# A sketched linear attention feeding a channel mix: k rows turned at unit stride, v in four loads, held loads, whole stationaries, and a new issue order

## The chip, the core and the metric

The kernel runs on one core of a Trainium2 chip. A core has five engines with a queue each, which run in their own order and meet only at semaphores: PE (matrix products, with a separate row for loading the stationary operand, PEld), DVE (vector), ACT (scalar functions), POOL (GpSimd) and SP (which here only starts transfers). A queue's instructions run in the order in which the program lists them. The metric is the time of one execution on the device in microseconds (us).

## What is computed

Four batches of four heads, 1088 positions, head width 32, sketch size 8. An attention with a product feature map, and a channel mix over its output:

```python
def phi(x):                       # (.., 32) -> (.., 64)
    a = np.einsum('rd,bhsd->bhsr', S1, x)
    b = np.einsum('rd,bhsd->bhsr', S2, x)
    return np.einsum('bhsi,bhsj->bhsij', a, b).reshape(*x.shape[:-1], r * r)
q_p, k_p = phi(q), phi(k)
kv, z = np.einsum('bhsf,bhsd->bhfd', k_p, v), np.sum(k_p, axis=2)
num = np.einsum('bhsf,bhfd->bhsd', q_p, kv)
den = np.einsum('bhsf,bhf->bhs', q_p, z)[..., None] + 1e-06
x = (num / den)                   # heads side by side: (4, 1088, 128)

x_prev = shift of x by one position, zero in front
xk, xr = mu_k * x + (1 - mu_k) * x_prev, mu_r * x + (1 - mu_r) * x_prev
k = np.maximum(xk @ w_k, 0.0)     # 128 -> 1024
out = 1 / (1 + np.exp(-(xr @ w_r))) * ((k * k) @ w_v)
```

## The kernel before

The program is a list of small tasks. Each is a Python function, and the string `ORDER` names them in the order in which they are issued; an engine runs its share of that list in list order. An entry such as `abev.0.1.A` is task, batch, part and engine (A for ACT, V for DVE, G for POOL, P for DVE reading straight from PSUM), and the digits behind `@` are the PSUM banks it writes. All eight banks are one tile; the framework inserts the semaphore waits for everything that shares a tile's region, a buffer or a bank.

Per batch, the attention goes through these tasks:

- `kt` (L260): DVE turns the k rows in 32x32 blocks, half a batch at a time, into `kT`; `qt` (L264) does the same for q.
- `kproj` (L269): PE projects the turned k with both sketches. `abev` copies the result to SBUF, `kp` (DVE or POOL) forms the 64 products of a position.
- `zmm`, `zev`, `wmm`, `wsq`: the sum over positions, folded into a third column block of `SQ[b]`, the right-hand side of q's projection, so that the denominator comes out of the same matmuls.
- `abw` (L346): PE projects q with `SQ[b]`: part `q` the two sketches, `w` the denominator's column, `f` all three. `pw` and `den` make the reciprocal of the denominator, `an` scales, `qp` forms the products.
- `kvmm`, `kvev`, `kdmm`, `kdev`: kv from `kp` and v, copied and turned into `kvw`.
- `pt`, `ptev`, `xp`, `xpev` (and `tt`, `ttev`, `xt`, `xtev` for the last two positions of each 34; `tr`, `xn`, `xnev` in the last batch): the q products turned and multiplied with kv, into `X32`, the channel mix's input.

The channel mix works in nine groups, two per batch and one (8) of the remainders of all batches: `xk` and `xr` mix with the position before; `f1` (L505) is the first matmul, in four parts of a pair of banks each, `relu` its activation, `sq` the square, `f2` the second matmul, `rr` and `sig` the gate, `fin` the product, `st` the store. `f1` and `xp` write two banks, which `pair` (L101) addresses as `PS[:, i:j + 1:j - i, :n]`, a strided region from the first bank to the last. In `st` the queues S and A are SP's and ACT's; with `SA` four transfers are shared between the two.

`muset` (L226) prepares the mixing coefficients with six small DVE instructions (L227 to L232). `wkset`, `wvset` and `wrset` cast the weights. `zz` are matmuls on zeros into a bank that is free, for PE's clock.

The loads are all started by SP in the order of the string `LOADS` before anything else on its queue, the small ones by ACT. k and q come as rows of 34 positions, one row per partition, 32 partitions per head; k's first load is in two halves. v comes in two loads per batch, to every second partition (L132 to L136). With k turned into `kT[P, 9, 32, 4]` at a stride of four elements, position 34a + 9c.. sits at column 4a + c, and v lies at the same partitions:

```python
nc.vector.transpose(_ap(kT[b % 2][:, 0, 0], [[1, 2], [128, 9], [4, 32]], 2 * y), ...)   # kt
d = o[32 * i:32 * i + 32, 32 * (m - m0):32 * (m - m0) + 32]                            # kproj, i in 0..3
kT[b % 2][:, m, 8 * i:8 * i + 8]                                                       # its stationary, 32 columns
```

In `kproj` and `abw` each group of 128 positions is projected by four matmuls whose stationaries have 32 columns, one for each strip of 32 output partitions.

Of the kernel before, what the change touches and what calls it, by code (L numbers as in the profile page):

```python
# [39 lines left out]
pt.1.1.1@7 kt.3.1 kproj.3.0@1 fin.0 kproj.3.1@0 abev.3.1.A f1.1.3@26 den.2.0.36 abev.3.0.A xk.0.2.G sq.1.0.V xr.0.1.V  # L40
kvmm.2.0@5 ptev.1.0.0.A relu.1.3.A an.2.0.36.G kp.3.1.G ptev.1.1.1.V zmm.3@7 zev.3.A kvmm.2.1 kvev.2.A xt.1 xp.1.0@04
sq.1.3.A xp.1.1@26 qt.3.1 kp.3.0.P wmm.3 xpev.1.0.A xtev.1.A qt.3.0 wsq.3 f2.1.0@1 sq.1.1.A xs.1.A abw.3.0.f@7
abwev.3.0.f.A xpev.1.1.V xk.1.1.P abw.3.1.f@3 xk.1.0.P rr.1@2 sig.1 f1.3.0@67 qp.2.20.36.G xr.1.0.P f2.1.1 f1.2.3@04
abwev.3.1.f.V f2.1.2 qp.2.0.20.G f1.2.0@23 relu.3.0.A relu.2.3.A f2.1.3 pw.3.0.36.V f1.3.1@67 sq.3.0.V pt.2.0.1@0
sq.2.3.V relu.2.0.A fin.1 xk.1.2.G xr.1.2.V kdmm.2 f1.3.2@23 sq.2.0.V den.3.0.36 relu.3.1.A f1.3.3@14 kdev.2.V
pt.2.0.0@6 ptev.2.0.0.V relu.3.2.A pt.2.1.1@7 f1.2.2@23 pt.2.1.0@5 relu.3.3.A f1.2.1@14 tt.2@6 ptev.2.1.1.V relu.2.2.A
ptev.2.1.0.A ptev.2.0.1.V relu.2.1.A ttev.2.V st.1.S kvmm.3.0@7 sq.3.2.V sq.3.1.A xp.2.0@05 sq.3.3.V xp.2.1@23
xpev.2.1.A xt.2 kvmm.3.1 xpev.2.0.V xtev.2.V sq.2.1.A rr.2@1 sig.2 xr.1.1.G f2.3.0@6 rr.3@4 an.3.0.36.G xs.2.V
qp.3.0.20.G kvev.3.V sig.3 xk.2.1.P f2.3.1 f1.5.0@23 relu.5.0.A xk.2.0.P xr.2.0.P xr.2.1.V f2.3.2 f1.5.2@14 sq.2.2.V
f2.3.3 fin.3 xk.2.2.G qp.3.20.36.G f1.4.0@23 relu.5.2.A f2.2.0@0 tr.3.0 kdmm.3 relu.4.0.A f1.4.3@16 relu.4.3.A f2.2.1  # L50
f1.4.2@23 f2.2.2 kdev.3.V xn.3.0@4567 sq.5.0.V tr.3.1 rr.5@1 f2.2.3 fin.2 relu.4.2.A f1.5.1@23 xnev.3.0.A xs.3.G
xk.3.0.V xn.3.1@4567 sq.5.2.V rr.4@0 sig.5 f2.5.0@1 relu.5.1.A f1.4.1@23 sq.5.1.V sq.4.0.V xnev.3.1.A f1.6.0@45
sq.4.3.V f1.5.3@67 sig.4 relu.4.1.A sq.4.1.V relu.5.3.A f2.5.1 st.3.S f2.4.0@0 relu.6.0.A f1.6.3@23 relu.6.3.A
xk.3.2.V f2.5.2 f1.6.2@67 sq.5.3.V f2.5.3 st.0.S f2.4.1 f1.6.1@45 sq.4.2.V relu.6.2.A xk.3.1.V fin.5 relu.6.1.A
# [555 lines left out]
```

## Time and profile before

| | us |
|---|---|
| runs before, median of 3 | 117.89 (117.11 to 118.21) |
| the profiled execution | 118.51 |
| its span in the profile | 116.7 |
| PE busy | 83.2 |
| DVE busy | 77.2 |
| ACT busy | 63.8 |
| POOL busy | 46.5 |

The span runs from the first recorded instruction to the last. Busy times are unions of instruction durations on one engine. In rows in order of time the columns are the start, the duration, the engine, the line, the operation, output and inputs with their shapes, the number of instructions merged in the row, and in brackets the idle time of that engine just before and what ended it. In rows by line stand the total busy time and the mean duration in ns, then the idle time before. `ACTq` and `SPq` rows are the issuing of transfers on those queues. A line can be that of a helper: L258 is every elementwise product, L251 and L255 the copies on ACT and DVE.

### The profile page before, as it was taken

Reading aid. Unit: us, or ns where it says so; the run is one execution under the profiler, and the core shown is the slowest. Engines: PE = TensorE matmul, PEld = TensorE weight load, DVE = VectorE, ACT = ScalarE, POOL = GpSimd, SP = SyncE. Lnnn points to the kernel's source line nnn. Section 1 sums busy time; section 2 is a strip of 40 time slices with the busy share of each in tenths; the row PEclk is TensorE's granted clock in tenths of the full one; section 3 lists DMA queues with packets and bytes.
Section 4 is the critical chain, followed back from the end, with each engine's and each line's share of the span. In section 5 each row is a group of like instructions: output and inputs, shape, how many; then the busy total and the mean of one; then the engine's idle time right before and its main releaser. Section 6 shows DMA issues by size and latency. Waiting matters only on the chain.

```text
span 116.7 us, 3943 instructions
## 1 busy us (share of the span) xinstructions
PE 83.2 (71%) x1720; PEld 60.9 (52%) x1731; DVE 77.2 (66%) x128; ACT 63.8 (55%) x93; POOL 46.5 (40%) x64
## 2 busy tenths in 40 slices
PE   5898391897199770877678369796298989968640
PEld 2294371776159650846556146466176656637540
DVE  4759987373783513961996459756696499996440
ACT  2212100269445775237857439797356899768450
POOL 6319341058649900150599900825200498000000
PEclk9999859589755999779999999999967999999999
DMA  3899999910000000000000001300015000145404
GB/s 106 268 318 402 389 397 388 370 51 6 0 6 0 0 8 0 0 0 6 3 6 6 0 0 22 68 6 3 6 34 133 19 0 0 27 102 132 102 5 132
DMA packets 9860, 10.27 MB, mean 88 GB/s; under 512 B 882, under 2 KB 7284, under 8 KB 9844
## 3 DMA queue, kind: packets, MB, share of 16 engines
q1 hardware_dynamic: 9232, 9.77, 25.8%
q10 hardware_dynamic: 612, 0.27, 1.0%
q8 instruction: 13, 0.21, 0.7%
q14 instruction: 3, 0.02, 0.1%
HBM read 7.80 MB, written 2.23 MB: 86 GB/s over the span
## 4 chain that ended last, share of the span: by engine, by line
PE 22%; DVE 17%; ACT 11%; SPq 4%; issue 3%; DMA 1%; ACTq 1%; DVEq 0%
ACT k L519 7%; PE ps L540 7%; DVE k L258 5%; PE ps L513 5%; SPq L568 4%; PE ps L431 3%; DVE q L558 3%; DVE xk L483 3%; PE ps L549 2%; DVE X L255 2%; ACT q L555 2%; PE ps L440 1%; DMA out_dram<-q 1%; DVE xr L483 1%; DVE xk L486 1%
## 5 line engine op out<-in xcount | busy, mean ns | idle before, releaser
L519 ACT ACTIVATE k<-ps 128x1024 bf16<-128x1024 f32 (+1 forms) x36 | 33.9, 976 | 18.7 <-PE ps L513 9.3
L540 PE MATMUL ps<-wv,k 128*128 128x128 bf16 x272 | 21.7, 227 | 7.2 <-ACT k L519 5.1
L540 PEld LDWEIGHTS <-k 128*128 128x128 bf16 x272 | 18.4, 102 | 13.9 <-issue 9.4
L513 PE MATMUL ps<-xk,wk 128*128 128x512 bf16 x54 | 18.0, 413 | 6.9 <-ACT k L519 3.2
L258 DVE TENSOR_TENSOR k<-k 128x1024 bf16<-128x1024 bf16 (+1 forms) x26 | 17.3, 701 | 4.0 <-ACT k L519 4.0
L258 POOL TENSOR_TENSOR qp<-an,abw 128x1280 f32<-128x1280 f32 (+3 forms) x9 | 16.6, 1857 | 0.2
L258 POOL TENSOR_TENSOR kp<-ab 128x1024 f32<-128x1024 f32 (+1 forms) x5 | 10.6, 2131 | 7.7 <-ACT ab L251 7.7
L513 PEld LDWEIGHTS <-wk 128*128 128x128 bf16 x72 | 6.4, 103 | 9.1 <-issue 5.2
L258 POOL TENSOR_TENSOR an<-abw,den 128x288 f32<-128x288 f32 (+2 forms) x5 | 3.3, 651 | 19.3 <-DVE den L384 13.0
L558 DVE TENSOR_TENSOR q<-ps,q 128x512 f32<-128x512 f32 (+1 forms) x9 | 5.9, 658 | 7.2 <-PE ps L540 3.6
L276 PE MATMUL ps<-SK,kT 128*32 128x64 f32 x288 | 7.7, 285 | 3.5 <-issue 2.8
L356 PE MATMUL ps<-SQ,qT 128*32 128x96 f32 (+2 forms) x360 | 8.3, 247 | 2.5 <-DVE SQ L314 2.0
L261 DVE STREAM_TRANSPOSE kT<-kv 128x576 f32<-128x576 f32 x8 | 9.4, 1194 | 1.0 <-DMA kv<-in_k_dram 1.0
L528 ACT ACTIVATE k<-k 128x1024 bf16<-128x1024 bf16 (+1 forms) x10 | 9.9, 1014 | 0.1
L276 PEld LDWEIGHTS ps<-SK,kT 128*32 128x32 f32 x288 | 6.8, 154 | 3.9 <-issue 2.9
L356 PEld LDWEIGHTS ps<-SQ,qT 128*32 128x32 f32 x360 | 6.9, 120 | 3.7 <-DVE SQ L314 2.6
L251 ACT COPY ab<-ps 128x320 f32<-128x320 f32 (+1 forms) x8 | 3.1, 400 | 10.2 <-PE ps L276 10.2
L431 PE MATMUL ps<-ident,qp 128*128 128x128 f32 x48 | 8.7, 324 | 0.1
L431 PEld LDWEIGHTS ps<-ident,qp 128*128 128x128 f32 x48 | 7.0, 170 | 1.5 <-issue 0.7
L483 DVE SCALAR_TENSOR_TENSOR xk<-ps,rat,X 128x512 bf16<-128x512 f32 x6 | 4.5, 750 | 4.6 <-ACT k L519 1.7
L258 DVE TENSOR_TENSOR kp<-ps,ab 128x1280 f32<-128x1280 f32 x3 | 4.4, 1476 | 4.6 <-ACT ab L251 4.6
L323 PE MATMUL ps<-kp,kv 128*32 128x64 f32 x288 | 6.8, 245 | 0.0
(95 smaller groups left out, 120.4 us busy)
## 6 DMA issues: line engine op xcount, KB each, us to landing
q<-in_q_dram SPq DMA_DIRECT2D x4, 544.0 KB, 7.7
out_dram<-q SPq DMA_DIRECT2D x28, 64.0 KB, 1.8
kv<-in_k_dram SPq DMA_DIRECT2D x3, 544.0 KB, 6.6
kv<-in_v_dram SPq DMA_DIRECT2D x4, 288.0 KB, 6.8
kv<-in_v_dram SPq DMA_DIRECT2D x4, 256.0 KB, 7.5
kv<-in_k_dram SPq DMA_DIRECT2D x2, 272.0 KB, 2.9
wk_f<-in_moe_w_k_dram SPq DMA_DIRECT2D x1, 512.0 KB, 9.2
wv_f<-in_moe_w_v_dram SPq DMA_DIRECT2D x1, 512.0 KB, 9.4
```

The lines of the kernel that those rows point to most:

```text
L258: (nc.gpsimd if eng == "G" else nc.vector).tensor_mul(o, x, y)
L261: nc.vector.transpose(_ap(kT[b % 2][:, 0, 0], [[1, 2], [128, 9], [4, 32]], 2 * y), kin[b][:, y].rearrange("p (c m d) -> p c m d", c=2, m=9))
L276: nc.tensor.matmul(_ap(d, [[n, 2], [1, 32]]), kT[b % 2][:, m, 8 * i:8 * i + 8].rearrange("p a c -> p (a c)"), SK[:].rearrange("p x h r -> ...
L323: nc.tensor.matmul(o[32 * h:32 * h + 32, :F], vin[b][:, h, m, :], sb["kp", b, j][:, 4 * (m - KG[j][0]) + h].rearrange("p i j -> p (i j)"), ...
L356: nc.tensor.matmul(_ap(o[32 * c:32 * c + 32], [[w * step, H], [1, w]], w * i0), qT[b % 2][:, 4 * t + c, :], SQ[b][:, :, R * x0:R * x1], sk ...
L431: nc.tensor.transpose(o[:, P * h:P * h + P], x.rearrange("p y i j -> p (y i j)"), ident[:])
L483: nc.vector.scalar_tensor_tensor(o.rearrange("p (y n) -> p y n", y=2), ps["xp", b, g], rat[:, i:i + 1], x[:, u:u + n].rearrange("p (y n) - ...
L513: nc.tensor.matmul(h[:, c, :], wk[:, 2 * cp + c].rearrange("p y f -> p (y f)"), x, skip_group_check=True)
L519: nc.scalar.activation(o[:, :, :size(g)], h, RELU)
L528: nc.scalar.activation(o[:, :, :n], k1[:, :, :n], mybir.ActivationFunctionType.Square)
L540: nc.tensor.matmul(o[:, i * P:i * P + P], k2[:, c, i * P:i * P + P], wv[:, 2 * cp + c, :], start=(cp == 0 and c == 0 and i == 0), stop=(cp ...
L558: nc.vector.tensor_mul(osb(g), ps["o", g][:, :size(g)], osb(g))
```

## The change

Four edits in the functions, and a new list of tasks.

`kT` becomes `[P, 9, 4, 32]` and `kt` writes 32 elements at unit stride, so that column 32c + a holds row a of chunk c. v is laid out to match: chunk c goes to partitions 32c to 32c+31 in a load of its own, four per batch in the order 0, 2, 1, 3.

An entry of `LOADS` with a plus sign is no load but a transfer of four bytes out of the named tile into `held`: SP can issue it only when that tile's load has landed, and what stands behind it on SP's queue is issued after it.

`kproj` and `abw` take a letter: T as before, four stationaries of 32 columns; W, one of 128 columns. Two of eight `kproj` and three of ten `abw` have W: `kproj.0.1`, `kproj.1.0`, `abw.0.1.q`, `abw.0.1.w` and `abw.1.1.f`, together 21 groups of positions.

```diff
-LOADS = "k0 q0 v0 k1 q1 w0 v1 w1 w2 k2 q2 v2 k3 q3 v3"
+LOADS = "k0 q0 k1 v0 +k1 q1 w0 +v0 v1 w1 w2 +v1 k2 q2 +q2 v2 k3 +v2 q3 v3"
...
     def load_v(b):
-        s = v[b].rearrange("h (p u) d -> p h u d", u=U // 2)
-        for y in range(2):
-            nc.sync.dma_start(vin[b][y::2, :, :9 - y, :].rearrange("p h m d -> p h (m d)"),
-                              s[:, :, 9 * y:17 if y else 9, :].rearrange("p h m d -> p h (m d)"))
+        s = v[b].rearrange("h (a u) d -> a h u d", u=U)
+        for c in (0, 2, 1, 3):
+            n = 9 - c % 2
+            nc.sync.dma_start(vin[b][32 * c:32 * c + 32, :, :n, :].rearrange("p h m d -> p h (m d)"),
+                              s[:, :, CU[c]:CU[c] + n, :].rearrange("a h m d -> a h (m d)"))
...
+    held = const.tile([1, 32], F32)
+    for i, x in enumerate(LOADS.split()):
+        x, b = x[-2], int(x[-1])
+        if LOADS.split()[i][0] == "+":
+            src = {"k": kin, "q": qin}[x][b][:1, 1, :1] if x in "kq" else vin[b][96:97, 0, 0, :1]
+            nc.sync.dma_start(held[:, i:i + 1], src)
+        elif x == "k":
...
-    kT = [const.tile([P, 9, 32, 4], F32, name=f"kT{i}") for i in range(2)]
+    kT = [const.tile([P, 9, 4, 32], F32, name=f"kT{i}") for i in range(2)]
...
-        nc.vector.transpose(_ap(kT[b % 2][:, 0, 0], [[1, 2], [128, 9], [4, 32]], 2 * y),
+        nc.vector.transpose(_ap(kT[b % 2][:, 0, 2 * y], [[32, 2], [128, 9], [1, 32]]),
...
+        w = 32 if how == "T" else P
         for m in range(m0, m1):
-            for i in range(4):
+            for i in range(0, P, w):
...
+                nc.tensor.matmul(_ap(o[i:i + w, 32 * (m - m0):32 * (m - m0) + 32], [[n, 2], [1, 32]]),
+                                 kT[b % 2][:, m].rearrange("p c a -> p (c a)")[:, i:i + w],
                                  SK[:].rearrange("p x h r -> p x (h r)"), skip_group_check=True,
-                                 tile_position=(0, 32 * i))
+                                 tile_position=(0, i) if w == 32 else None)
```

`abw` is changed in the same way. Of the list, 397 entries long (398 before), these are the parts of which the prediction speaks: the start, the feed-forward of batch 0, and the end.

```diff
-kt.0.0 zz.5@7 smm@0 sset zz.3@1 mumm@0 kt.0.1 zmu@1 kproj.0.0@2 abev.0.0.A kproj.0.1@3 abev.0.1.A sqset zset qt.0.1
-qt.0.0 zz.2@1 zmm.0@3 zev.0.A zz.1@2 wmm.0 abw.0.0.q@2 abwev.0.0.q.A kp.0.0.G muset wsq.0 abw.0.1.w@3 abw.0.0.w@0
-kt.1.1 kp.0.1.G pw.0.0.20.P den.0.0.20 abw.0.1.q@2 kvmm.0.0@1 zz.1@0 kvmm.0.1 kvev.0.A an.0.0.20.G kt.1.0 kproj.1.0@0
-abev.1.0.A qp.0.0.8.V qt.1.0 kproj.1.1@4 abev.1.1.A abwev.0.1.q.V qp.0.8.20.G kdmm.0 kp.1.1.G pt.0.0.0@5 ptev.0.0.0.A
...
-ttev.0.V pw.0.20.36.P den.0.20.36 an.0.20.36.G xp.0.0@46 xpev.0.0.A xt.0 xtev.0.V abw.1.0.f@3 abwev.1.0.f.A
-abw.1.1.f@2 abwev.1.1.f.A xs.0.G xk.0.0.P f1.0.0@05 xr.0.0.P qp.0.20.28.G relu.0.0.A f1.0.2@37 qp.0.28.36.G
...
-relu.0.3.A sq.0.1.A sq.0.3.A abw.2.1.f@2 kp.2.1.G abw.2.0.f@6 wvset.1.V sq.0.2.A kdev.1.A xpev.0.1.V xk.0.1.P
-abwev.2.0.f.V kt.3.0 tt.1@3 f2.0.1 pt.1.0.1@0 abwev.2.1.f.V pw.2.0.36.G ttev.1.V ptev.1.0.1.A xr.0.2.G pt.1.1.0@6
...
-st.6.SA f1.8.1@67 relu.8.1.A sq.8.1.V f1.8.3@15 rr.7@2 sig.7 f2.7.2 f2.8.0@6 sq.8.2.V relu.8.3.A sq.8.3.A f2.7.3 fin.7
-f2.8.1 xr.2.2.G rr.8@2 sig.8 st.7.SA f2.8.2 f2.8.3 fin.8 st.8.S
+zz.6@7 smm@0 kt.0.0 zmu@1 sset sqset kt.0.1 zz.1@2 mumm@0 muset kproj.0.0.T@2 abev.0.0.V qt.0.0 zset qt.0.1
+kproj.0.1.W@3 abev.0.1.A zz.2@0 zmm.0@3 zev.0.A zz.1@2 wmm.0 kp.0.0.G kp.0.1.G abw.0.1.q.W@1 kt.1.0 abw.0.0.q.T@2
+abwev.0.0.q.A wsq.0 abw.0.0.w.T@3 abwev.0.1.q.A kt.1.1 kproj.1.1.T@0 abev.1.1.A abw.0.1.w.W@2 pw.0.0.20.P den.0.0.20
+an.0.0.20.G qp.0.0.8.G kproj.1.0.W@1 abev.1.0.A kp.1.1.P qt.1.1 kvmm.0.0@0 pw.0.20.36.P den.0.20.36 qp.0.8.20.G
...
+wkset.0.A abw.1.1.f.W@1 abwev.1.0.f.A kdev.0.V wkset.1.V wvset.1.V pt.0.0.1@4 abwev.1.1.f.A pw.1.0.36.V ptev.0.0.0.A
+ptev.0.0.1.A den.1.0.36 an.0.20.36.G kt.2.1 qp.0.20.28.G qp.0.28.36.G pt.0.1.0@0 ptev.0.1.0.A pt.0.1.1@1 ptev.0.1.1.A
+wrset.G xt.0 xtev.0.A kt.2.0 xs.0.A xp.0.0@24 xpev.0.0.A kvmm.1.0@5 xp.0.1@01 xpev.0.1.A kvmm.1.1 kproj.2.0.T@3
+abev.2.0.A xk.0.0.P f1.0.1@24 kproj.2.1.T@6 wvset.0.G xk.0.1.P xr.0.1.P abev.2.1.V f1.1.0@37 relu.0.1.A relu.1.0.A
+kvev.1.V qt.2.1 an.1.0.36.G qp.1.0.20.G qp.1.20.36.G f1.1.2@01 relu.1.2.A f1.1.1@24 qt.2.0 kp.2.0.G pt.1.0.1@6
+ptev.1.0.1.V zmm.2@3 zev.2.V sq.1.0.A relu.1.1.A pt.1.0.0@7 sq.0.1.A kdmm.1 kdev.1.A f1.0.0@01 kt.3.0 wmm.2 wsq.2
...
+xr.3.0.G st.5.S sq.8.0.V rr.6@5 sig.6 sig.7 fin.6 st.6.SA f2.7.1 f1.8.3@17 f1.8.2@36 relu.8.2.A f2.7.2 f2.8.0@5
+sq.8.2.V f2.7.3 fin.7 st.7.SA xr.2.2.G relu.8.3.A f2.8.1 rr.8@3 f2.8.2 sq.8.3.A f2.8.3 sig.8 fin.8 st.8.S
```

More of the change, by code (lines that the diff above doesn't have):

```diff
@@ L40 @@
[L40 to L54, printed above, removed]
@@ new lines @@
+pt.1.1.0@6 kt.3.1 abw.2.0.f.T@3 relu.0.0.A ptev.1.0.0.V ptev.1.1.0.V f1.0.2@24 relu.0.2.A abwev.2.0.f.V pt.1.1.1@7
+ptev.1.1.1.V abw.2.1.f.T@5 abwev.2.1.f.V xk.0.2.V f1.0.3@36 relu.0.3.A kproj.3.0.T@0 kp.2.1.G f1.1.3@57 f2.1.0@2
+qt.3.0 pw.2.0.36.G qt.3.1 kproj.3.1.T@4 sq.0.2.V abev.3.0.A rr.1@3 sq.1.2.V relu.1.3.A abev.3.1.A tt.1@6 kvmm.2.0@1
+zmm.3@4 sq.1.1.A ttev.1.A kvmm.2.1 sig.1 kvev.2.A xp.1.0@57 xr.0.0.V zev.3.V xt.1 xtev.1.A den.2.0.36 xpev.1.0.V
+xs.1.A sq.1.3.A wmm.3 f2.1.1 wsq.3 rr.0@6 f2.1.2 sig.0 xk.1.0.P kp.3.1.G abw.3.0.f.T@4 xr.0.2.G sq.0.0.A xr.1.0.P
@@ new lines @@
+ptev.2.1.1.V relu.3.2.A sq.3.0.A kvev.3.V xt.2 xtev.2.V pt.2.1.0@7 ptev.2.1.0.A f2.2.0@4 f1.3.1@26 relu.3.1.A
+qp.3.20.36.G f2.2.1 xpev.2.0.V xs.2.V xp.2.1@57 xk.2.0.P f1.4.1@13 xpev.2.1.A relu.4.1.A kdmm.3 f2.2.2 tr.3.0
+f1.4.0@57 relu.4.0.A kdev.3.V tr.3.1 f2.2.3 fin.2 xn.3.0@0123 xk.2.1.G xnev.3.0.A f1.4.2@57 f2.3.0@6 sq.3.3.V xs.3.G
+rr.3@0 relu.4.2.A sq.3.1.V xn.3.1@1234 sig.3 f1.5.0@57 sq.4.0.V xnev.3.1.A f2.3.1 f1.4.3@12 relu.5.0.A sq.3.2.V
+relu.4.3.A f2.3.2 f1.5.1@57 relu.5.1.A f2.3.3 sq.4.1.V sq.4.2.V f1.5.2@34 f2.4.0@1 xk.3.0.V fin.3 st.3.S f1.5.3@02
@@ L267, with kproj @@
     KG = ((0, 5), (5, 9))
-    def kproj(b, j, banks):
+    def kproj(b, j, how, banks):
         o = ps["ab", b, j] = PS[:, banks[0], :]
@@ L347, with abw @@
     S0 = (0, 20, 36)
-    def abw(b, g, part, banks):
+    def abw(b, g, part, how, banks):
         o = ps["abw", b, g, part] = PS[:, banks[0], :]
```

33 lines of the change are left out of this document (17 added, 16 removed).

## The prediction

> **What bounds the kernel now.** I read the page's sums first, then the busy time by stage, the order of time, and last the rows by line.
>
> ```profile
> span 116.7 us, 3943 instructions
> PE 83.2 (71%) x1720; PEld 60.9 (52%) x1731; DVE 77.2 (66%) x128; ACT 63.8 (55%) x93; POOL 46.5 (40%) x64
> core 0: us, PE busy (x) PEld busy (x) DVE busy (x) ACT busy (x) POOL busy (x), PEclk, DMA share, GB/s
> 3.50:28.60 25.10, 19.24 (x568) 15.02 (x569) 18.22 (x30) 6.84 (x16) 11.04 (x16) 0.86 0.82 294
> 30.00:70.00 40.00, 26.94 (x597) 20.21 (x601) 24.15 (x36) 22.90 (x35) 20.30 (x20) 0.87 0.01 2
> 75.00:110.00 35.00, 28.39 (x492) 20.26 (x496) 26.29 (x42) 25.65 (x34) 10.49 (x11) 0.95 0.18 41
> ```
>
> No engine fills the span. PE is busy 81% of the stage from 75 to 110 us (28.39 of 35), 67% from 30 to 70 (26.94 of 40). So the end is set by waits between engines, and mostly by those of the first 70 us. The order of time shows two of them.
>
> ```profile
> 8.42 4.31 POOL L258 TENSOR_TENSOR kp<-ab 128x1280 f32<-128x1280 f32 x2 [2.68 <-ACT ab L251]
> 8.75 2.10 DVE L228 TENSOR_SCALAR omu<-mu 128x2 f32<-128x2 f32 x1
> 10.88 1.88 DVE L229 TENSOR_SCALAR tmp<-omu 128x2 f32<-128x2 f32 x1
> 12.79 0.16 DVE L230 TENSOR_TENSOR omu<-omu,tmp 128x2 f32<-128x2 f32 x1
> 13.26 0.18 DVE L314 TENSOR_TENSOR SQ<-ps,m 128x32 f32<-128x32 f32 x1
> 16.04 0.46 POOL L258 TENSOR_TENSOR an<-abw,den 128x160 f32<-128x160 f32 x1 [3.31 <-DVE den L384]
> 28.65 0.75 DVE L483 SCALAR_TENSOR_TENSOR xk<-ps,rat,X 128x512 bf16<-128x512 f32 x1 [1.60 <-ACT X L251]
> 29.45 0.38 PE L513 MATMUL ps<-xk,wk 128*128 128x512 bf16 x1 [1.10 <-DVE xk L483]
> ```
>
> The first: two DVE instructions on two elements (muset, L228 and L229) take 2.10 and 1.88 us, where their neighbour L230 takes 0.16. They end at 10.85 and 12.76; POOL's two kp run from 8.42 to 12.73. They stood still while POOL worked, 3.98 - 2x0.16 = 3.7 us, and wsq (L314) with pw, den and POOL's an came behind them. The first feed-forward matmul (f1, L513) starts only at 29.45.
>
> ```profile
> 42.37 2.94 ACT L528 ACTIVATE k<-k 128x1024 bf16<-128x1024 bf16 x3
> 45.21 0.25 ACT L251 COPY kvw<-ps 128x128 f32<-128x128 f32 x1
> 45.50 0.69 DVE L255 COPY X<-ps 128x512 f32<-128x512 f32 x1 [4.18 <-ACT kvw L251]
> 46.23 0.75 DVE L483 SCALAR_TENSOR_TENSOR xk<-ps,rat,X 128x512 bf16<-128x512 f32 x1
> 47.12 0.38 PE L450 MATMUL ps<-ident,qp 64*64 64x64 f32 x4 [3.56 <-DVE xk L483]
> 49.14 0.80 POOL L258 TENSOR_TENSOR pw<-abw 128x288 f32<-128x288 f32 x1 [8.40 <-DVE abw L255]
> ```
>
> The second: three squares hold ACT, kdev.1 waits behind them, and then DVE idles 4.18 us, PE 3.56 and POOL 8.40. xpev.0.1 (DVE, banks 0 and 4) waits for kdev.1 (bank 1), with which it shares no bank, and tt.1 (PE, bank 3) for the reader of 0 and 4. From this I take it that a pair of banks keeps out whatever touches a bank between the two.
>
> **The front.** The new order puts muset ahead of the first kproj, hence ahead of POOL's first kp: the 3.7 us of DVE go, on the path to an. These rows price what else changes there:
>
> ```profile
> L261 DVE STREAM_TRANSPOSE kT<-kv 128x576 f32<-128x576 f32 x8 | 9.4, 1194 | 1.0 <-DMA kv<-in_k_dram 1.0
> L265 DVE STREAM_TRANSPOSE qT<-q 128x544 f32<-128x544 f32 x8 | 5.7, 723 | 0.3 <-DMA q<-in_q_dram 0.3
> L258 DVE TENSOR_TENSOR kp<-ps,ab 128x1280 f32<-128x1280 f32 x3 | 4.4, 1476 | 4.6 <-ACT ab L251 4.6
> L258 DVE TENSOR_TENSOR qp<-an,abw 128x512 f32<-128x512 f32 x1 | 1.8, 1814 | 0.0
> L255 DVE CAST wv<-wv_f 128x512 bf16<-128x512 f32 x1 | 0.4, 417 | 0.0
> L258 DVE TENSOR_TENSOR pw<-abw 128x288 f32<-128x288 f32 x1 | 0.5, 457 | 0.0
> L276 PE MATMUL ps<-SK,kT 128*32 128x64 f32 x288 | 7.7, 285 | 3.5 <-issue 2.8 <-ACT k L519 0.7
> L310 PE MATMUL ps<-zs,ZL 128*128 128x32 f32 x8 | 1.4, 260 | 0.0
> ```
>
> A k turn writes at a stride of four elements and takes 1194 ns for 576; a q turn writes at unit stride and takes 723 for 544. At unit stride the k turn should take 723x576/544 = 765, a saving of 0.43 us. No row shows that block shape, so the saving lies between 0 and 0.43; I take 0.43, as the q turn differs in little else.
> DVE's list up to xk.0.0, L483 at 28.65: it loses muset's 3.7, four dearer turns (1.7) and qp.0.0.8, which goes to POOL (1.8). It gains kp.1.1 from POOL (1476x1024/1280 = 1.2), two turns of batch 2 (1.5), wkset.1 and wvset.1 (0.4 each by the cast), pw.1 (0.46) and den.1 (an estimate of 0.9, two instructions of pw's size or so). That is -7.2 + 4.9 = -2.3. The old front was 25.1 us with DVE busy 18.2, so 6.9 of gaps. With the old gaps xk.0.0 comes 2.3 us earlier. But the old list made DVE wait for POOL and ACT behind the stalled muset, and what it waited for now starts 3.7 us earlier; with gaps of 4 it is 5.2. I take **-4**.
>
> Beside that path: 21 projection units run with one whole stationary instead of four strips. Four strips cost 7.7 us/36 = 0.21 us of PE a unit; the nearest whole fp32 stationary, L310, costs two instructions of 1.4/8 us, 0.35 a unit. That bounds the addition at 21x0.14 = 3 us, and from below at about -1 if fewer instructions help. PE has 5.9 us of gaps in that stage, and most of the units wait for DVE. I take 0; without the gaps it is up to +1 on the path. POOL takes qp.0.0.8 in its gaps (11.04 busy of 25.1). wkset.1 on DVE could stand still behind a POOL instruction as muset did: 0 to 1 us; POOL should be through qp by then.
>
> **The loads.** Five reads of four bytes each hold SP until a load has landed, and queued behind each are the next k, q, v and w loads; v is issued in four pieces.
>
> ```profile
> 9.27 0.56 SPq L130 DMA_DIRECT2D kv<-in_k_dram  x1
> 11.82 3.26 SPq L135 DMA_DIRECT2D kv<-in_v_dram  x2
> L135 SPq DMA_DIRECT2D kv<-in_v_dram x8: 612/615/672, 2.4 to 18.0; - x8
> kv<-in_k_dram SPq DMA_DIRECT2D x3, 544.0 KB, 6.6
> kv<-in_k_dram SPq DMA_DIRECT2D x2, 272.0 KB, 2.9
> 12.00:24.00 12.00, 7.68 (x271) 6.46 (x272) 8.93 (x16) 1.16 (x4) 3.64 (x4) 0.72 1.01 371
> ```
>
> k1 moves ahead of v0, 544 KB at 371 GB/s or 1.5 us earlier. A hold costs nothing if another load is still in flight, at most the 2.9 us from issue to landing on an empty queue. Four pieces at 0.615 take SP 2.5 us for 544 KB that the queue moves in 1.5, so 1 us more for a v. k2, issued at 9.27, landed about 15.9 (9.27 + 6.6); three holds and two v loads stand ahead of it, so it lands at 16 to 27 (15.9 + 3x2.9 + 2x1). kt.2.1 wants it at about 21. I take 20, so no cost, and the late end as a rival. SP stores nothing before 70 us.
> The Trainium skill ("SBUF — State Buffer", section "Door 1: The DMA port swizzle") says that partitions 0 to 31 reach only eight of sixteen ports, and gives 189 GB/s there. By that an estimate for a v is 2.9 us; two of them ahead of k2 would add 2.8 instead of the 2 above and leave the sum alone unless the holds cost as well. No run yet shows such a load.
>
> **The middle.** xk.0.1, at 46.2 in the old run, now follows xk.0.0 directly, so both halves of batch 0 can feed PE. kdev.1 now has one square directly ahead of it, and xpev.0.1 is on ACT and no longer behind it. The eight f1 pairs of batch 0 took banks 05 37 24 37 47 12 06 26, 37 banks counting those between; now 24 37 01 24 01 24 36 57, 25. If nothing is gained the term is 0. If the stage from 30 to 70 packs PE as the one from 75 to 110 does, it takes 26.94/0.81 = 33.3 us instead of 40: -6.7. I take **-4**, about the 4.18 us that DVE stood. DVE's cheaper turns lie under that cover.
>
> **The tail.**
>
> ```profile
> 110.81 0.60 ACT L519 ACTIVATE k<-ps 128x512 bf16<-128x512 f32 x1
> 111.44 0.63 ACT L528 ACTIVATE k<-k 128x512 bf16<-128x512 bf16 x1
> 112.18 1.19 DVE L558 TENSOR_TENSOR q<-ps,q 128x512 f32<-128x512 f32 x2 [0.95 <-PE ps L540]
> 112.90 0.86 ACTq L568 DMA_DIRECT2D out_dram<-q  x2
> 113.79 0.40 SPq L564 DMA_DIRECT2D out_dram<-q  x1
> ```
>
> In the old tail relu.8.3 and sq.8.3 were done when fin.7 came; fin.8 followed at once (both in the row at 112.18), and 1.6 us after fin.7 began, the last store was issued (113.79). Now ACT has st.7's two issues (0.86, waiting for fin.7) ahead of relu.8.3 (0.60) and sq.8.3 (0.63); f2.8.3 and fin.8 wait for these. That adds 0.86 + 0.60 + 0.63 = 2.1 us, 0 if fin.7 comes early for another reason. I take **+2**.
>
> **Sum:** -4 - 4 + 2 = -6. The profiled execution took 118.5 (116.7 span and 1.8 around it), 0.6 above the runs' median of 117.9: 111.9 on the median's scale.
>
> **Rivals.**
> - *The middle packs fully* (-6.7, front -5.2, tail +1): -11, 107. For it: no engine is above 70% there. Against: the old order left it so.
> - *The turn is no cheaper*: six turns in the front, +2.6: 114.5.
> - *The holds gate the front.* k2 comes at 26, DVE stands 5 us at kt.2.1 with xk.0.0 behind it; front +1, middle half (-2), tail +2: +1, 118.9. For it: the hold drains the queue. Against: w1 and w2 are in flight at the hold for v1.
> - *Slower: ACT's queue.* With eight relus and five squares of batch 0 back to back, the short copies for batches 2 and 3 (abev.3, kvev.2, xtev.1) stand behind 1 us instructions, and DVE, PE and POOL wait as they did at 42 to 49. Two such places of 4.18 us and no gain in the middle: -4 + 8.4 + 2 = +6.4, 124; one place: 120. It decides once it costs over 2 us more than the old waits. For it: ACT was idle before most of those copies, and won't be. Against: fewer squares and copies of z are on ACT now.
>
> **Numbers.** About 1% is what a measurement can tell here (runs lie from 117.1 to 118.2). Forecast 0.45, own range 108.5 to 115 (the terms' ends cut where all go one way); full packing 0.12; dear turn 0.12; holds 0.11, of which 0.09 within 1%; ACT's queue 0.20. Faster 0.45 + 0.12 + 0.12 = 0.69; within 1% 0.09; slower 0.22. The range 105.5 to 121.5 leaves out about half of the packing and of the ACT case, 0.16.
>
> **What would show it.** Right: L228 and L229 at about 0.2 us before 7 us, L261 at 0.77, POOL's an before 13 us, the first L513 at 24 to 26, eight relus of batch 0 done by 50. Wrong: a DVE wait on k2's load before L261; POOL or DVE idle over 4 us behind an ACT copy between 30 and 60; the first f1 after 28 us. No ACTq issue in front of the last relu on the chain would void the tail's term.

## The result and the profile after

| | before, us | after, us |
|---|---|---|
| runs, median of 4 each | 117.50 (117.00 to 118.21) | 127.47 (126.29 to 129.13) |
| the profiled execution | 118.51 | 127.39 |
| its span in the profile | 116.7 | 125.6 |

Medians are taken over all runs of a kernel; a ratio with an interval is taken from its fast runs alone, those within 1.5% of its fastest. The changed kernel is slower: 1.081 times the time of before (95% interval 1.070 to 1.092). The forecast was 111.9, its range 105.5 to 121.5. In the changed program L267, L271 and L264 are the old L261, L265 and L258 (k turn, q turn, products), L282 and L364 the projections of k and q, L523, L529 and L550 are f1, relu and f2 (before L513, L519 and L540), L568 is fin and L159 the held read.

The sums and the same three stages as before:

```profile
span 125.6 us, 3716 instructions
PE 88.4 (70%) x1592; PEld 64.0 (51%) x1603; DVE 76.1 (61%) x133; ACT 61.5 (49%) x91; POOL 50.0 (40%) x60
```

```profile
3.50:28.60 25.10, 23.88 (x535) 19.53 (x536) 15.87 (x36) 8.37 (x22) 15.78 (x20) 1.00 0.71 219
30.00:70.00 40.00, 29.53 (x627) 20.88 (x630) 26.52 (x44) 24.59 (x34) 16.46 (x13) 0.91 0.20 56
75.00:110.00 35.00, 24.60 (x338) 16.96 (x343) 23.07 (x34) 20.67 (x27) 12.01 (x11) 0.84 0.14 32
```

The columns are those of the same table in the prediction. In the first two stages PE is busy for longer than before (23.88 us against 19.24, 29.53 against 26.94), in the first of them with fewer matmuls (535 against 568). In the last it gets less done: 338 matmuls from 75 to 110 us where the old kernel ran 492. The first matmuls of the channel mix (f1, 72 in all) count the progress. Some matmul records are missing from both traces, so their weight loads (PEld) are counted, of which all 72 are there. First the kernel before, by L513, then the changed one, by L523; the number in brackets is how many ran in the stretch.

```profile
3.00:50.00 47.00, 1.13 (x10) 0.83 0.45 161
50.00:80.00 30.00, 1.86 (x22) 0.98 0.05 11
80.00:140.00 60.00, 3.44 (x40) 0.95 0.14 34
```

```profile
3.00:50.00 47.00, 1.39 (x16) 1.00 0.54 162
50.00:80.00 30.00, 1.49 (x16) 0.79 0.08 19
80.00:140.00 60.00, 3.51 (x40) 0.89 0.12 30
```

At 50 us the new order is ahead, 16 to 10. At 80 us both stand at 32, and from there the new one needs 46 us, the old one 37, for the same 40. So the change did gain in this count as far as 50 us, and lost more behind it, in a place of which the prediction says nothing. The waits after 50 us show what it lost to. Columns: who waited for whom, the total in us, how often, the longest. Before, and then after:

```profile
PE ps L540 <- ACT k L519: 5.1, 6, 1.1
ACT k L519 <- PE ps L540: 4.7, 4, 1.9
DVE q L558 <- PE ps L540: 3.6, 2, 2.6
```

```profile
PE ps L550 <- ACT k L529: 17.2, 14, 2.4
DVE q L568 <- PE ps L550: 9.9, 6, 3.1
ACT k L529 <- PE ps L550: 9.3, 8, 3.1
```

f2 waits for a relu 14 times and a relu for f2 8 times. Neither reads what the other writes: f2 reads the squares, relu reads f1's banks. They can meet only in PSUM's banks. Three of these waits in a row, ACT's part of the order of time:

```profile
58.15 1.02 ACT L529 ACTIVATE k<-ps 128x1024 bf16<-128x1024 f32 x1 [2.02 <-PE ps L550]
62.25 1.02 ACT L529 ACTIVATE k<-ps 128x1024 bf16<-128x1024 f32 x1 [3.08 <-PE ps L550]
65.22 1.94 ACT L529 ACTIVATE k<-ps 128x1024 bf16<-128x1024 f32 x2 [1.95 <-PE ps L550]
```

The list has `f1.2.2@24`, `f2.0.1`, `relu.2.2.A`, `f1.2.3@16`, `f2.0.2`, `relu.2.3.A`, `f1.3.0@24`, `f2.0.3`, `relu.3.0.A` there, with f2.0's sum in bank 3. Relu reads banks 2 and 4, or 1 and 6; bank 3 lies between them, and relu waits for the f2 ahead of it, as the next f2 then waits for relu.

### The profile page after: what moved, and what is told of

Its sections match the earlier page's. It is cut to its first block, busy times and chain, and to the rows that moved or that the text cites. A ratio compares the mean times of both kernels' runs of the same rounds, so it can differ in the third digit from the quotient of the medians.

```text
span 125.6 us, 3716 instructions
## 1 busy us (share of the span) xinstructions
PE 88.4 (70%) x1592; PEld 64.0 (51%) x1603; DVE 76.1 (61%) x133; ACT 61.5 (49%) x91; POOL 50.0 (40%) x60
## 4 chain that ended last, share of the span: by engine, by line
PE 51%; DVE 21%; ACT 17%; issue 7%; ACTq 2%; another core or an unknown queue 0%; DVEq 0%
ACT k L529 15%; PE ps L550 14%; PE ps L364 8%; PE ps L523 8%; DVE k L264 7%; PE ps L282 6%; DVE q L568 4%; PE ps L191 3%; PE ps L330 3%; PE ps L450 3%; DVE XT L491 2%; PE ps L441 2%; DVE kv L261 1%; ACTq L578 1%; DVE xk L493 1%
## 5 line engine op out<-in xcount | busy, mean ns | idle before, releaser
L529 ACT ACTIVATE k<-ps 128x1024 bf16<-128x1024 f32 (+1 forms) x36 | 34.4, 976 | 35.8 <-PE ps L523 13.2
L550 PE MATMUL ps<-wv,k 128*128 128x128 bf16 x272 | 23.9, 240 | 17.3 <-ACT k L529 17.2
L550 PEld LDWEIGHTS <-k 128*128 128x128 bf16 x272 | 20.5, 109 | 28.0 <-issue 25.4
L523 PE MATMUL ps<-xk,wk 128*128 128x512 bf16 x54 | 19.8, 437 | 8.1 <-ACT k L529 3.0
L264 DVE TENSOR_TENSOR k<-k 128x1024 bf16<-128x1024 bf16 (+1 forms) x28 | 21.5, 815 | 5.6 <-ACT k L529 5.6
L264 POOL TENSOR_TENSOR qp<-an,abw 128x512 f32<-128x512 f32 (+3 forms) x10 | 18.4, 1855 | 8.2 <-DVE an L264 7.9
L568 DVE TENSOR_TENSOR q<-ps,q 128x512 f32<-128x512 f32 (+1 forms) x9 | 5.9, 660 | 16.2 <-PE ps L550 9.9
L264 POOL TENSOR_TENSOR kp<-ab 128x1024 f32<-128x1024 f32 (+1 forms) x5 | 10.6, 2132 | 4.6 <-ACT ab L257 2.4
L364 PE MATMUL ps<-SQ,qT 128*32 128x96 f32 (+5 forms) x288 | 11.1, 265 | 1.3 <-ACT k L529 1.0
L364 PEld LDWEIGHTS ps<-SQ,qT 128*32 128x32 f32 (+1 forms) x288 | 9.5, 137 | 2.7 <-ACT k L529 1.3
L523 PEld LDWEIGHTS <-wk 128*128 128x128 bf16 x72 | 6.4, 107 | 8.1 <-issue 6.4
L282 PE MATMUL ps<-SK,kT 128*32 128x64 f32 (+1 forms) x234 | 8.5, 259 | 0.3
L282 PEld LDWEIGHTS ps<-SK,kT 128*32 128x32 f32 (+1 forms) x234 | 7.2, 140 | 1.1 <-issue 1.0
L257 ACT COPY ab<-ps 128x256 f32<-128x256 f32 (+1 forms) x6 | 2.4, 398 | 9.1 <-PE ps L282 9.1
L267 DVE STREAM_TRANSPOSE kT<-kv 128x576 f32<-128x576 f32 x8 | 5.9, 752 | 1.2 <-DMA kv<-in_k_dram 1.2
L261 DVE COPY X<-ps 128x512 f32<-128x512 f32 (+1 forms) x4 | 2.3, 570 | 6.3 <-ACT k L529 3.7
L565 ACT ACTIVATE q<-ps 128x512 f32<-128x512 f32 (+1 forms) x9 | 5.1, 573 | 1.6 <-PE ps L559 1.6
```

The lines of the kernel that those rows point to most:

```text
L264: (nc.gpsimd if eng == "G" else nc.vector).tensor_mul(o, x, y)
L267: nc.vector.transpose(_ap(kT[b % 2][:, 0, 2 * y], [[32, 2], [128, 9], [1, 32]]), kin[b][:, y].rearrange("p (c m d) -> p c m d", c=2, m=9))
L282: nc.tensor.matmul(_ap(o[i:i + w, 32 * (m - m0):32 * (m - m0) + 32], [[n, 2], [1, 32]]), kT[b % 2][:, m].rearrange("p c a -> p (c a)")[:, ...
L364: nc.tensor.matmul(_ap(o[c:c + m], [[w * step, H], [1, w]], w * i0), qT[b % 2][:, 4 * t:4 * t + 4, :].rearrange("p u a -> p (u a)")[:, c:c ...
L523: nc.tensor.matmul(h[:, c, :], wk[:, 2 * cp + c].rearrange("p y f -> p (y f)"), x, skip_group_check=True)
L529: nc.scalar.activation(o[:, :, :size(g)], h, RELU)
```

## The experiments

Each ran beside the kernel before on the same chip, whose median there was 115.85 to 116.85. Where an interval stands, it is that of the ratio to those runs. Not all experiments ran on one chip, so differences between two of them are less certain than the ratios. One of the 13 runs of the kernel before that stood beside three of the experiments (muset alone; banks and muset; banks, strips and tail) took 238.18 us, the other twelve 114.23 to 119.47.

**Only the banks renamed.** Every bank number of the changed list is replaced by a permutation (0 1 3 2 4 7 5 6). Which steps share a bank stays; what changes is which banks lie between the two of a pair. As a measure I counted on the list the steps that some other engine's step, at most 12 entries ahead, holds back by a bank in between and by no shared one. It is a count on the list, which no profile shows; with slightly different rules the numbers shift (106 where 112 stands below, 54 for 46, 165 for 177), so take its order and not its price.

```diff
-f2.1.3 f1.2.0@57 abwev.3.0.f.A sq.0.3.V kdmm.2 relu.2.0.A kdev.2.A abw.3.1.f.T@6 fin.1 st.1.S f1.2.1@24 relu.2.1.A
-f2.0.0@3 an.2.0.36.G qp.2.0.20.G kp.3.0.P xp.1.1@57 kvmm.3.0@0 abwev.3.1.f.V sq.2.0.A xpev.1.1.V xk.1.1.P f1.2.2@24
+f2.1.3 f1.2.0@67 abwev.3.0.f.A sq.0.3.V kdmm.2 relu.2.0.A kdev.2.A abw.3.1.f.T@5 fin.1 st.1.S f1.2.1@34 relu.2.1.A
+f2.0.0@2 an.2.0.36.G qp.2.0.20.G kp.3.0.P xp.1.1@67 kvmm.3.0@0 abwev.3.1.f.V sq.2.0.A xpev.1.1.V xk.1.1.P f1.2.2@34
```

> The changed kernel with its banks renamed throughout (2 and 3 change places, 5 becomes 7, 6 becomes 5, 7 becomes 6), nothing else: the pairs most used become neighbours. Theory A (a pair keeps out what touches a bank between its two, and the new list puts second matmuls there): PE's wait of L550 for ACT L529 falls from 17.2 us to under 8, time 112 to 119 us. Rival B (whole stationaries) and rival C (held loads): nothing changes, 126 to 129 us.

111.7 us (108.16 to 113.92, 4 runs), 15.8 less than the changed kernel by the medians; its slowest run is 12.4 us below the fastest run of the changed kernel (126.29). The same three relus, now on banks 3 and 4 or 1 and 5, with f2.0 in bank 2:

```profile
53.81 1.02 ACT L529 ACTIVATE k<-ps 128x1024 bf16<-128x1024 f32 x1 [0.30 <-PE ps L523]
55.14 1.02 ACT L529 ACTIVATE k<-ps 128x1024 bf16<-128x1024 f32 x1 [0.30 <-PE ps L550]
56.84 1.94 ACT L529 ACTIVATE k<-ps 128x1024 bf16<-128x1024 f32 x2 [0.68 <-PE ps L523]
```

7.05 us of ACT's waits have become 1.28. The one of the three that still waits for f2 (55.14) is on banks 1 and 5, with bank 2 in between. By 80 us 45 of the 72 weight loads of f1 have run, against 32. After 50 us, f2 waits for relu 4 times instead of 14:

```profile
PE ps L550 <- ACT k L529: 5.8, 4, 2.0
```

**Strips instead of whole stationaries**, all 21 units, on the changed list (`kproj.0.1.W` to `.T` and so on).

> The changed kernel with strips of 32 columns everywhere (every W made T). Rival B: the whole stationaries cost some 3.6 us of PE in the front; the first L523 comes at 26 us instead of 29.8 and the time falls by 3 us or more, to 124 or below; if they were the whole cause, to 118. Theory A: the front gets shorter but the list after 50 us waits on itself as before, so 124 to 127 us.

128.22 us (125.71 to 128.84): no gain, and 1.2 above the range of theory A. POOL's an came at 13.94 instead of 16.11, yet the first f1 stayed at 30.00. The earlier an isn't shown to come from the strips: PE also ran faster here from the start (a weight load of 32 columns in k's projection took 110 ns against 171; see the last section). In between PE stood still for nothing that the profile names (releaser "issue"):

```profile
12.34 0.23 PE L364 MATMUL ps<-SQ,qT 128*32 128x32 f32 x3 [1.62 <-issue]
17.61 0.75 PE L330 MATMUL ps<-kp,kv 128*32 128x64 f32 x19 [2.15 <-issue]
```

**No held reads** on the changed list.

```diff
-LOADS = "k0 q0 k1 v0 +k1 q1 w0 +v0 v1 w1 w2 +v1 k2 q2 +q2 v2 k3 +v2 q3 v3"
+LOADS = "k0 q0 k1 v0 q1 w0 v1 w1 w2 k2 q2 v2 k3 q3 v3"
```

> The changed kernel without the five held reads, loads in the same order. Rival C (held loads starve the front): time 121 us or less. Theory A: no engine but the first turn waits for a load in the changed kernel's trace, so 126 to 129 us, with the loads done by about 25 us instead of 37.

130.79 us (128.22 to 131.18), not faster, and 1.8 above the range of theory A. The loads were done by about 28 us, where 25 was expected and about 39 was measured with the holds. The holds are not what slows the kernel; whether they help by a per cent or two stays open, since this and the changed kernel weren't run side by side.

**The old list and loads order with the new layout** (turn at unit stride, v in four loads, strips).

> The list and the load order of before, with k turned at unit stride and v in four loads to 32 partitions each, all strips. Theory A: the layout does no harm; the turns take 0.75 us instead of 1.19, time 115 to 118 us. Rival D (four v loads to 32 partitions are slow and starve the kernel): 119 us or more.

118.84 us (117.16 to 120.82), the kernel before 115.85 there (114.88 to 119.13): the layout alone brings nothing. That lies between the ranges of theory A (115 to 118) and of rival D (119 or more): by the medians it is 3 us slower, the two ranges overlap, and whether the four v loads cost something stays open. The turn took 759 ns in it, so 8 x 0.43 us of DVE went without showing in the total.

**The banks further apart.** The changed list again, with the permutation that leaves most banks in between (177 by the count).

```diff
-xr.1.2.G xk.1.2.V pw.3.0.36.V xr.1.1.P f2.0.1 relu.2.2.A f1.2.3@16 f2.0.2 relu.2.3.A f1.3.0@24 f2.0.3 relu.3.0.A
+xr.1.2.G xk.1.2.V pw.3.0.36.V xr.1.1.P f2.0.1 relu.2.2.A f1.2.3@26 f2.0.2 relu.2.3.A f1.3.0@14 f2.0.3 relu.3.0.A
```

> The changed kernel with its eight banks renamed once more, now so that as many pairs as possible have another bank in use between them; which steps share a bank, the order, the loads and all instructions stay. Counted on the list, 177 steps are put behind another engine by a bank that only lies between (112 in the changed kernel, 46 in the kernel of the renaming that gave 111.7). Theory A (a pair of banks keeps out what touches a bank between them, and that is what costs): about 0.24 us a step from those two (15.8 us for 66 steps), so 127 + 0.24 x 65 = 143, at least over 132; PE's wait on ACT's relu before f2 stays at 17 us or grows. Theory B (the first renaming won by another effect of the numbers, for instance by where it put single tiles): no relation with the count, 108 to 130.

138.64 us (two runs; ratio 1.194, 1.176 to 1.213). Slower as expected of theory A, 4 us less than its line. In one point the expectation missed: f2's wait for relu did not stay the largest (7.8 us); the time went into other pairs of the same kind, with single waits up to 6.4 us:

```profile
ACT k L529 <- PE ps L550: 12.3, 4, 6.4
DVE q L568 <- PE ps L550: 11.2, 5, 3.0
```

**Renamed banks, and st.7's issues moved.**

```diff
-sq.8.2.V f2.7.3 fin.7 st.7.SA xr.2.2.G relu.8.3.A f2.8.1 rr.8@2 f2.8.2 sq.8.3.A f2.8.3 sig.8 fin.8 st.8.S
+sq.8.2.V f2.7.3 fin.7 xr.2.2.G relu.8.3.A f2.8.1 rr.8@2 f2.8.2 sq.8.3.A sig.8 st.7.SA f2.8.3 fin.8 st.8.S
```

> The kernel with renamed banks (111.7 before), and st.7's two issues on ACT moved behind sq.8.3 and sig.8. The prediction's tail term: the issues hold relu.8.3, sq.8.3, f2.8.3 and fin.8 behind fin.7. From fin.7's start to the last store's issue took 4.1 us there (105.36 to 109.45); without the wait relu.8.3 follows relu.8.2 directly and this falls to about 2.0. If the term is right, 111.7 - 2 = 109.7. Rival: the last stores' landing or DVE's list sets the end, and it stays within 0.5 of 111.7.

108.76 us (108.47 to 109.58; ratio 0.938, 0.929 to 0.948). By the medians that is 2.9 less than 111.7, but one of the four runs there took 108.16, so how much of it is gain isn't clear of the spread. The end of the changed kernel, and of this one:

```profile
118.75 0.69 DVE L568 TENSOR_TENSOR q<-ps,q 128x512 f32<-128x512 f32 x1 [0.46 <-PE ps L550]
119.47 0.86 ACTq L578 DMA_DIRECT2D out_dram<-q  x2
120.43 0.60 ACT L529 ACTIVATE k<-ps 128x512 bf16<-128x512 f32 x1 [2.60 <-DVE q L568]
122.89 0.35 SPq L574 DMA_DIRECT2D out_dram<-q  x1
```

```profile
103.22 0.68 DVE L568 TENSOR_TENSOR q<-ps,q 128x512 f32<-128x512 f32 x1
103.93 0.86 ACTq L578 DMA_DIRECT2D out_dram<-q  x2
104.99 0.35 SPq L574 DMA_DIRECT2D out_dram<-q  x1
```

From fin.7 to the last store's issue took 4.1 us (118.75 to 122.89), with relu.8.3 behind ACT's two issues, and now takes 1.8 (103.22 to 104.99).

**The kernel before with renamed banks**, by (1 0 7 6 3 2 4 5), nothing else: 55 by the count instead of 104.

```diff
-qp.3.0.20.G kvev.3.V sig.3 xk.2.1.P f2.3.1 f1.5.0@23 relu.5.0.A xk.2.0.P xr.2.0.P xr.2.1.V f2.3.2 f1.5.2@14 sq.2.2.V
+qp.3.0.20.G kvev.3.V sig.3 xk.2.1.P f2.3.1 f1.5.0@67 relu.5.0.A xk.2.0.P xr.2.0.P xr.2.1.V f2.3.2 f1.5.2@03 sq.2.2.V
```

> The kernel before with nothing but its banks renamed: steps ordered only by a bank that lies between go from 104 to 55 by the count on its list, PE behind ACT from 32 to 22. Theory A at 0.24 us a step: 12 us at most, but its list was slower from other waits too (the end of the chain goes through copies and squares held on ACT's queue), so I expect half: 112, range 108 to 115. Theory B, or a list whose bound lies elsewhere: 116 to 118, no change.

108.13 us (107.08 to 109.12; ratio 0.929, 0.917 to 0.940), a gain of 8.6 us where the middle value expected 4.7, and just inside the range. The old kernel had the same fault, unseen.

**Renamed banks and strips.**

> The kernel with renamed banks (111.7 before), with all 21 whole-stationary units turned back into four strips. If whole stationaries cost time on the path that sets the end: POOL's an comes 2 us earlier (13.9 against 16.0) and the total falls by 1 to 2, 110. If the strips only give the time back (PE issues about 250 instructions more in the front, and its stalls there each end 1.3 to 1.6 us behind a packet of the instruction queue), first f1 stays at 30 or later and the total at 111 to 114.

110.46 us (108.04 to 112.66). POOL's an came at 13.87, the first f1 at 29.08. The runs are too far apart to tell 110.5 from 111.7, and the an decides nothing either: with whole stationaries it came at 16.04 in the trace with renamed banks alone, where PE ran slowly in the front, and at 12.45 in the one with the tail moved as well, where it didn't.

**Only muset moved, in the kernel before.**

```diff
-kt.0.0 zz.5@7 smm@0 sset zz.3@1 mumm@0 kt.0.1 zmu@1 kproj.0.0@2 abev.0.0.A kproj.0.1@3 abev.0.1.A sqset zset qt.0.1
-qt.0.0 zz.2@1 zmm.0@3 zev.0.A zz.1@2 wmm.0 abw.0.0.q@2 abwev.0.0.q.A kp.0.0.G muset wsq.0 abw.0.1.w@3 abw.0.0.w@0
+kt.0.0 zz.5@7 smm@0 sset zz.3@1 mumm@0 kt.0.1 zmu@1 muset kproj.0.0@2 abev.0.0.A kproj.0.1@3 abev.0.1.A sqset zset qt.0.1
+qt.0.0 zz.2@1 zmm.0@3 zev.0.A zz.1@2 wmm.0 abw.0.0.q@2 abwev.0.0.q.A kp.0.0.G wsq.0 abw.0.1.w@3 abw.0.0.w@0
```

> The kernel before with one step moved: muset stands ahead of kproj.0.0 instead of behind kp.0.0, banks and all else as before. If the prediction's front step is right: L228 and L229 fall from 2.10 and 1.88 to about 0.2 us each, wsq.0 and pw come 3.7 us earlier, POOL's an at about 12.5 instead of 16.0, and the total falls by 2 to 4 (113 to 115 beside 116.7). If what stands behind it is gated by something else (PE's stall on its instruction queue at 18 to 21, the loads of k1), an comes earlier and the first f1 stays at 28 to 29.5: 116 to 117.

117.15 us in 10 runs, ratio 1.007 (0.995 to 1.019): nothing. The stall is gone (L228 at 5.92 takes 0.17 us), and the profile shows what came instead:

```profile
13.09 0.70 PE L356 MATMUL ps<-SQ,qT 128*32 128x32 f32 x36 [3.06 <-issue]
14.69 0.46 POOL L258 TENSOR_TENSOR an<-abw,den 128x160 f32<-128x160 f32 x1 [3.12 <-DVE den L384]
19.51 1.72 PE L276 MATMUL ps<-SK,kT 128*32 128x64 f32 x55 [3.33 <-issue]
29.39 0.39 PE L513 MATMUL ps<-xk,wk 128*128 128x512 bf16 x1
```

PE stood twice, 3.06 and 3.33 us, before the an and before k's projection for batch 1, and the first f1 came at 29.39 as ever. PE's busy time and matmuls between the two stops:

```profile
13.09:16.18 3.09, 2.63 (x127) 1.00 1.07 401
```

127 matmuls with a weight load each make 254 instructions between the stops. The transfer queue named "instruction" moved 13 packets, 0.21 MB, in the whole execution, so 16 KB each. One began at 10.82 for 0.95 us and the next at 17.02 for 1.09; PE went on 1.3 and 1.4 us after their ends. The longer stops named "issue" of the other kernels' fronts end 1.3 to 1.6 us behind such a packet too.

The place of the stops says the same. In every kernel with strips whose front has both, the first stands behind 443 of PE's instructions (matmuls and weight loads, counted in the rows in order of time) and the second behind 696 to 698: at 13.09 and 19.51 us here, 14.08 and 20.79 with banks and muset, 12.34 and 17.61 in the changed list in strips. In the changed list with whole stationaries, renamed banks and the tail, they stand behind 693 (19.46 us) and 945 (27.00). What PE does next differs from list to list; the steps of about 250 instructions don't. So PE waited for its own program.

**Both on the kernel before, banks and muset.**

> The kernel before with renamed banks (108.1) and muset moved as well. If the two gains are separate, 108.1 - 2 to 4 = 104 to 106. If the front is gated behind muset by something else, 108.

108.63 us (108.38 to 110.29; ratio 0.944, 0.928 to 0.961): muset again brings nothing that shows on top of 108.13.

**Renamed banks, strips and the tail** on the changed list.

> The changed kernel with renamed banks, strips throughout and st.7 behind sq.8.3 (each of the last two alone on top of the renaming: 110.5 and 108.8, beside 111.7). If the whole stationaries cost 1 us of the path and the tail 2: 107.5. If the strips only moved PE's stalls: 108.8.

106.63 us (105.50 to 108.56; ratio 0.920, 0.904 to 0.936), below both values expected, the lowest median of all, and 21 us below the changed kernel.

**Fewer PE instructions in the front.** The kernel with banks and muset, and q's projections of batches 0 and 1 with whole stationaries:

```diff
-            for c in range(4):
-                nc.tensor.matmul(_ap(o[32 * c:32 * c + 32], [[w * step, H], [1, w]], w * i0), qT[b % 2][:, 4 * t + c, :],
-                                 SQ[b][:, :, R * x0:R * x1], skip_group_check=True, tile_position=(0, 32 * c))
+            m = P if b < 2 else 32
+            for c in range(0, P, m):
+                nc.tensor.matmul(_ap(o[c:c + m], [[w * step, H], [1, w]], w * i0),
+                                 qT[b % 2][:, 4 * t:4 * t + 4, :].rearrange("p u a -> p (u a)")[:, c:c + m],
+                                 SQ[b][:, :, R * x0:R * x1], skip_group_check=True,
+                                 tile_position=(0, c) if m == 32 else None)
```

> The kernel before with renamed banks and muset moved (108.6), and the projections of q of batches 0 and 1 (27 units) with one whole stationary instead of four strips: 12 instructions fewer on PE a unit (each fp32 product is two multiplies and two weight loads), 324 in all, so more than one packet of 256. Theory: in the front PE waits for its own instructions (2.74 us before 20.79 and 1.68 before 14.08 there; in the kernel with muset moved alone 127 multiplies and 128 weight loads ran between two such stops). One stop falls away or both move later, POOL's an comes at 12.5 to 14 instead of 15.69 and the first f1 1.5 to 3 us before 29.50, less up to 2.7 us of dearer units on PE (0.02 to 0.16 each by the rows of the two kinds): total 106 to 108.2. Rival (the stops are something else, a load or a bank): both stops stay where they stand in the list, and the total rises by what the whole units cost, 109 to 111.

108.34 us (104.71 to 109.77): the median did not move from 108.63. But one of the four runs took 104.71, below every run without the edit, so whether the total can gain stays open. Both stops are gone. In order of time without the edit, and with it:

```profile
11.03 1.37 PE L356 MATMUL ps<-SQ,qT 128*32 128x64 f32 x107
14.08 1.13 PE L356 MATMUL ps<-SQ,qT 128*32 128x32 f32 x37 [1.68 <-issue]
20.79 1.56 PE L276 MATMUL ps<-SK,kT 128*32 128x64 f32 x55 [2.74 <-issue]
```

```profile
11.01 7.92 PE L357 MATMUL ps<-SQ,qT 128*128 128x64 f32 x36
```

And PE's busy time from 9 to 22 us, again without and with:

```profile
9.00:22.00 13.00, 8.23 (x308) 0.83 1.06 395
```

```profile
9.00:22.00 13.00, 13.00 (x152) 1.00 1.06 395
```

Half the matmuls, and PE busy for all 13 us. The 18 units of batch 0 take 2.5 us in strips (144 matmuls in the first two rows) and 7.92 whole: 0.14 and 0.44 us each. POOL's an even came later, at 18.51 against 15.69, and the first f1 at 29.57 against 29.50.

These two prices aren't taken at one pace. PE ran slowly in this front: the first record of the granted clock stands at 23 us, and at 11 in the trace without the edit. The kernel with renamed banks and tail has both kinds of unit at one faster pace. Whole units with 64 columns, first here (9 units of two matmuls) and then there (4 units), and there units in strips (5 units of eight):

```profile
L357 PE MATMUL ps<-SQ,qT 128*128 128x64 f32 x18 | 4.3, 425 | 0.0
```

```profile
L364 PE MATMUL ps<-SQ,qT 128*128 128x64 f32 x8 | 1.1, 277 | 0.0
L364 PE MATMUL ps<-SQ,qT 128*32 128x64 f32 x40 | 0.8, 221 | 0.0
```

That is 0.48, 0.28 and 0.16 us a unit. At one pace a whole unit costs 0.12 more, within the 0.16 expected; the rest of the 0.30 is the slow PE. A slow PE also uses its instructions up more slowly, so this run alone doesn't show that the stops went because the instructions became fewer; that they stand at fixed counts of instructions does.

## Why the prediction was wrong

**The middle (-4) is the step that failed**, and its sign with it. Its own sign of success came true: 8 relus ran by 50 us, 4 in the old kernel. But the term lets that lead last to the tail, and the sum has nothing for what stands between; there the lead was lost, and 9 us more. The mechanism behind it was right: a pair of banks does keep out what touches a bank between. It was read off the old trace from two waits (xpev.0.1 for kdev.1, tt.1 for its reader), and then applied to eight f1 pairs, those of batch 0, which span 25 banks instead of 37. There are 36 such pairs. Over all of them only 5 are neighbours in the new list, where 20 were before, and the prediction did not look at which bank f2's sum holds meanwhile: from batch 1 on the list puts it between the two of the next pair. The same count for the whole list gives 112 for the changed kernel and 104 before, 51 and 32 of them PE behind ACT. With nothing changed but the names, the changed list takes 111.7 us at 46, 127.5 at 112 and 138.6 at 177, and the old one 108.1 at 55 and 116.7 at 104. That is shown and settles the cause; the price of a single such wait isn't constant (by this count 0.24 us a step from 46 to 112, 0.17 from 112 to 177). PE's pace in the front doesn't explain it: in the traces of the changed kernel and of the one with only the banks renamed the first record of the clock stands at 16.0 us and POOL's an at 16.1 and 16.0.

The number of such steps alone doesn't make the new list slower than the old one (112 and 104); by the names the new list loses 15.8 us and the old one 8.6, so it is which steps they are. With the banks renamed in both and the tail mended the two stand at 108.8 and 108.1 us: what else the change did, by its sum, brought nothing that shows.

The Trainium skill ("PSUM — Partial Sum Buffer", section "PSUM bank collisions raise a hardware error ⚠️") has engines kept apart by bank, and within it by groups of 32 partitions. By that rule a bank in between needs no wait at all, and the trace with renamed banks agrees as far as it goes: there f2 writes bank 2 from 53.62 to 54.23 us while relu reads banks 3 and 4 from 53.81 to 54.83. So I take it that the waits come from the framework, to which a strided pair would be one region from its first bank to its last; its code isn't shown here.

**The front (-4)** gave nothing by the clock time of the first f1, 29.83 against 29.45. Its parts on DVE were sized well: muset's stall went (0.17 and 0.17 us), the k turn fell to 752 ns where 765 was worked out, and DVE never waited for k2.

```profile
6.12 0.17 DVE L234 TENSOR_SCALAR omu<-mu 128x2 f32<-128x2 f32 x1
6.32 0.17 DVE L235 TENSOR_SCALAR tmp<-omu 128x2 f32<-128x2 f32 x1
16.11 0.46 POOL L264 TENSOR_TENSOR an<-abw,den 128x160 f32<-128x160 f32 x1 [4.05 <-ACT ab L257]
29.83 0.38 PE L523 MATMUL ps<-xk,wk 128*128 128x512 bf16 x1 [1.36 <-DVE xk L493]
```

```profile
L267 DVE STREAM_TRANSPOSE kT<-kv 128x576 f32<-128x576 f32 x8 | 5.9, 752 | 1.2 <-DMA kv<-in_k_dram 1.2
```

What failed is the conclusion that DVE's list is the path. PE was the next bound, in both forms: with strips it waits for its instructions (6.4 us in the kernel with muset alone), with whole stationaries it works through them (busy 23.88 of 25.1 us). The latter is in part the slow PE of that execution. In the trace with renamed banks and tail PE ran faster from 4 us on; there POOL's an came at 12.45, before the 13 us that the prediction asked for, and the first f1 still only at 28.13, behind a stop of 2.05:

```profile
27.00 0.59 PE L330 MATMUL ps<-kp,kv 128*32 128x64 f32 x27 [2.05 <-issue]
```

The prediction took the "issue" of 2.8 us in the old row of L276, which it quoted, for a gap that could be filled, and it took whole stationaries at 0 with 3 us as the bound. Part of the missing gain is no loss: by its first f1 the new list has also issued work of batches 1 and 2 that the old one had behind it.

**The tail (+2)** was right in mechanism, and in size by the traces: fin.7 to the last issue grew from 1.6 to 4.1 us, and fell to 1.8 with the two issues moved. What that gives back in the total is 2.9 us by the medians, and not clear of the spread of the runs.

**The loads (0)** were about right: without the holds the kernel is no faster, and DVE waited for no load but the first; a few per cent for the four pieces stay open. The prediction's other price for a v, 2.9 us at the 189 GB/s that the Trainium skill ("SBUF — State Buffer", section "Door 1: The DMA port swizzle") gives for a transfer to partitions 0 to 31, isn't borne out. In the one stretch where only the four pieces of a v moved, they came to 297 GB/s together; in the old list with the new layout, where q and k loads fill the rest, the queues moved 352 GB/s from 15 to 20 us, against 392 before:

```profile
27.50:28.50 1.00, 1.00 0.97 297
```

**The rivals.** The slower one (ACT's queue, 120 to 124) had the sign and not the mechanism: ACT was busy 49% of the span, less than before, and it was itself made to wait. The one in which the turn is no cheaper is refuted, and the holds did not gate the front (the changed kernel's turns of k2, at 24.99 us, waited for no load).
